# Idle TensorE matmuls regrouped and three small loads moved to another queue, in the head of an attention-and-MLP kernel

## The chip, the cores and the metric

One core of a Trainium2 chip runs the whole program. The metric is the device time of one execution in microseconds (us); unless it says otherwise, a number is the median of several executions. The profile's span is about 2 us shorter than the device time (297.5 against 299.37 for the profiled execution of the kernel before). In the clock records of these traces TensorE's granted clock is either 1.00 or 0.50; "the clock gate is open" means 1.00, "closed" 0.50. In the views PE is TensorE, ACT is ScalarE, DVE is VectorE, POOL is GpSimd, and SP is SyncE, which only issues DMAs here.

## The reference

A linear attention with cosine position weights, whose output goes through a two-layer MLP:

```python
# q, k, v: (8, 8, 576, 64) fp32; w_in (512, 2048); w_out (2048, 512)
r = relu(x);  phi(x) = concat([r * cos_w, r * sin_w])        # 128 features per head
kv  = einsum('bhsf,bhsd->bhfd', phi(k), v)
num = einsum('bhsf,bhfd->bhsd', phi(q), kv)
den = einsum('bhsf,bhf->bhs', phi(q), sum_s phi(k)) + 1e-6
x   = (num / den).transpose(0, 2, 1, 3).reshape(4608, 512)
h   = x @ w_in
out = (h * sigmoid(1.702 * h)) @ w_out
```

## The kernel before

The tokens go through the MLP in nine blocks of 512. While the MLP of block i runs, the attention of batch i+1 is worked in between its matmuls. A batch has 576 tokens: four chunks of 128 and a tail of 64. Before block 0 stands a head in which only batch 0's attention can run. Nearly all loads are issued by GpSimd, which casts fp32 to bf16 on the way:

```python
for g in range(1, 4): load_w_in(g)
load_w_out(0)
for n in "qk":
    load_main(1, n)
    load_tail(1, n)          # 64 tokens of batch 1, cast to bf16 by GpSimd's queue
load_w_out(1)
load_main(1, "v")
load_tail(1, "v")
load_w_out(2); load_w_out(3)
load_all(2)                  # q, k, v of batch 2, the last of the first stream of loads
```

Idle matmuls on a zero tile keep TensorE (PE) busy while it waits:

```python
warmup(14)                   # 14 idle matmuls of 512 columns
...                          # k prepared; two chunks of q prepared and transposed on PE
kv_lo = mm_tile()
for _ in range(6):
    nc.tensor.matmul(kv_lo, warm[:, 0:128], warm, start=True, stop=True)   # six more
kv_half(0, 0, kv_lo)         # k^T v of batch 0, heads 0 to 3
```

At the end of block 0 the attention result of batch 1 must be transposed (`x` to `xT`) before block 1 can start. Chunks 2 and 3 go through PE, the others through a DMA transpose on the SP queue:

```python
for c, k in enumerate(ks):
    at(k, unit_num, b, c)
    if i == 0 and c in (2, 3):
        at(min(k + 2, 31), turn_x_at, b, c)     # on PE, copied by ScalarE (ACT)
    else:
        at(k, turn_x, b, c)                     # nc.sync.dma_start_transpose(...)
```

## Time and profile before

| | before |
|---|---|
| device time | 300.03 us (299.83 to 300.39, 4 runs) |
| span | 297.5 us |
| first transposes of q on PE | 11.07 us |
| first numerator (needs k^T v) | 16.62 us |
| block 1 starts | 57.57 us |

One more place matters, and the prediction did not look at it: how block 1 starts. This is PE's timeline of the kernel before there (start, length, engine, line, operation, operands, count, and in brackets the idle time before it and what ended it):

```profile
56.51 0.39 PE L203 MATMUL at<-ident,xb 128*128 128x128 bf16 x4
57.57 0.81 PE L251 MATMUL mm<-xT,w_in_sb 128*128 128x512 bf16 x3 [0.67 <-ACT xT L205]
```

These are the two DMA transposes of x, chunks 0 and 1 of batch 1, in the view of one source line (count, duration on the issuing queue in ns, first and last start in us, and the time from issue to landing):

```profile
L208 SPq DMA_TRANSPOSE xT<-xb x1: 1192/1192/1192, 52.0 to 52.0; - x1
DMA to landing us min/median/max: 3.4/3.4/3.4
...
L208 SPq DMA_TRANSPOSE xT<-xb x1: 1702/1702/1702, 53.2 to 53.2; - x1
DMA to landing us min/median/max: 4.1/4.1/4.1
```

The second one lands at 57.4 (53.23 + 4.15, unrounded). The profile names ACT's copy as what released block 1 at 57.57, but this transfer landed only 0.2 us earlier.

### The profile page before, as it was taken

The page shows a single profiled execution, that of the slowest core. Times are in us where ns is not written, and L with a number is a line of the kernel's source. Part 1 is how long each engine was busy: PE and PEld are TensorE (multiplying, and loading weights), DVE is VectorE, ACT ScalarE, POOL GpSimd, SP SyncE. Part 2 cuts the span into 40 slices and gives each one's busy share as a digit, 9 for nine tenths or more (in the row PEclk, how much of TensorE's full clock was granted, in tenths as well). Part 3 has the DMA queues.
Part 4 walks back from the last instruction along what each step waited for, and adds up shares of the span by engine and source line. Part 5 has one row for each costly group of instructions (what it writes and reads, how often), then busy time and mean ns, then how long its engine had stood idle before and what let it go on. Part 6 is the DMA issues. An engine that isn't in the chain of part 4 may idle for free.

```text
span 297.5 us, 4997 instructions
## 1 busy us (share of the span) xinstructions
PE 284.1 (96%) x1930; PEld 143.7 (48%) x1930; DVE 105.0 (35%) x349; ACT 119.6 (40%) x203; POOL 101.1 (34%) x116
## 2 busy tenths in 40 slices
PE   6588999899999999999999999999999999999994
PEld 2364455445544554455445544554455444444443
DVE  3850547851581158114821482148214200000000
ACT  5546610464126511751165116511651167127411
POOL 8541520492269015800590159004501200120021
PEclk9599999999999999999999999999999999999999
DMA  8999999889969965897799889994902710111033
GB/s 193 196 204 194 196 201 192 175 198 161 164 137 189 186 106 138 180 187 104 147 183 168 123 101 181 177 164 119 192 0 54 126 42 0 39 71 35 2 68 73
DMA packets 90935, 39.91 MB, mean 134 GB/s; under 512 B 59744, under 2 KB 88672, under 8 KB 90912
## 3 DMA queue, kind: packets, MB, share of 16 engines
q0 software_dynamic: 42896, 26.88, 60.2%
q1 hardware_dynamic: 47856, 12.59, 21.5%
q8 instruction: 15, 0.25, 0.3%
q10 hardware_dynamic: 160, 0.13, 0.2%
q14 instruction: 8, 0.07, 0.1%
HBM read 36.70 MB, written 9.44 MB: 155 GB/s over the span
## 4 chain that ended last, share of the span: by engine, by line
PE 92%; DMA 3%; DVE 2%; ACT 1%; SPq 0%; issue 0%; DVEq 0%
PE mm L251 41%; PE mm L286 40%; PE at L235 3%; PE at L215 3%; DMA vt<-in_v_dram 3%; PE mm L310 1%; PE mm L358 1%; PE mm L328 1%; DVE xb L243 1%; PE mm L375 1%; ACT xT L354 1%; PE at L197 1%; PE mm L352 0%; DVE inv L242 0%; SPq L86 0%
## 5 line engine op out<-in xcount | busy, mean ns | idle before, releaser
L286 PE MATMUL mm<-w_out_sb,g 128*128 128x512 bf16 x560 | 129.0, 379 | 0.0
L251 PE MATMUL mm<-xT,w_in_sb 128*128 128x512 bf16 x564 | 124.3, 379 | 0.7 <-ACT xT L205 0.7
L298 POOL DMA_DIRECT2D out_dram<-ysb x54 | 56.0, 1042 | 170.9 <-ACT ysb L296 169.5
L256 ACT ACTIVATE g<-mm 128x512 bf16<-128x512 f32 x144 | 85.6, 597 | 46.2 <-PE mm L251 45.7
L251 PEld LDWEIGHTS <-w_in_sb 128*128 128x128 bf16 x564 | 54.7, 98 | 65.2 <-issue 0.8
L286 PEld LDWEIGHTS <-g 128*128 128x128 bf16 x560 | 52.0, 98 | 56.6
L296 ACT COPY ysb<-mm 128x512 f32<-128x512 f32 x34 | 19.9, 586 | 111.9 <-PE mm L286 111.9
L219 DVE CAST kvs<-at 128x260 bf16<-128x260 f32 x14 | 5.4, 426 | 59.2 <-PE at L215 59.2
L243 DVE TENSOR_TENSOR xb<-at,inv 128x512 bf16<-128x512 f32 (+1 forms) x36 | 24.8, 689 | 1.2
L241 DVE TENSOR_SCALAR den<-at 128x8 f32<-128x8 f32 (+1 forms) x36 | 5.9, 165 | 52.0 <-PE at L235 52.0
L315 DVE COPY ysb<-mm 128x256 f32<-128x256 f32 x1 | 0.4, 424 | 59.4 <-PE mm L310 59.4
L235 PEld LDWEIGHTS <-qT 128*128 128x128 bf16 x280 | 13.5, 98 | 8.3 <-DVE xb L243 0.3
L235 PE MATMUL at<-kvs,qT 128*128 128x65 bf16 x280 | 14.6, 193 | 0.1
L181 DVE TENSOR_SCALAR kp<-k,cosw 128x512 bf16<-128x512 bf16 (+1 forms) x32 | 11.6, 370 | 3.7 <-DMA k<-in_k_dram 3.7
L215 PEld LDWEIGHTS <-kp 128*128 128x128 bf16 x320 | 11.0, 98 | 2.2 <-issue 0.6
L181 DVE TENSOR_SCALAR qn<-q,cosw 128x512 bf16<-128x512 bf16 x32 | 11.3, 354 | 0.0
L181 DVE TENSOR_SCALAR qn<-q,sinw 128x512 bf16<-128x512 bf16 x32 | 10.8, 337 | 0.0
L215 PE MATMUL at<-vt,kp 128*128 128x65 bf16 x280 | 9.6, 193 | 0.0
L181 DVE TENSOR_SCALAR kp<-k,sinw 128x512 bf16<-128x512 bf16 x28 | 9.4, 337 | 0.0
L77 POOL DMA_DIRECT2D v<-in_v_dram x9 | 8.0, 887 | 4.1 <-DMA v<-in_v_dram 2.3
L77 POOL DMA_DIRECT2D q<-in_q_dram x8 | 7.9, 988 | 1.4 <-POOLq L470 0.8
L242 DVE RECIPROCAL inv<-den 128x8 f32<-128x8 f32 (+1 forms) x36 | 7.2, 201 | 1.2
(69 smaller groups left out, 119.4 us busy)
## 6 DMA issues: line engine op xcount, KB each, us to landing
out_dram<-ysb POOLq DMA_DIRECT2D x38, 128.0 KB, 2.8
q<-in_q_dram POOLq DMA_DIRECT2D x8, 512.0 KB, 9.1
out_dram<-ysb POOLq DMA_DIRECT2D x16, 256.0 KB, 3.1
k<-in_k_dram POOLq DMA_DIRECT2D x7, 512.0 KB, 11.0
v<-in_v_dram POOLq DMA_DIRECT2D x7, 512.0 KB, 12.5
w_out_sb<-in_moe_w_out_dram POOLq DMA_DIRECT2D x4, 512.0 KB, 15.2
w_in_sb<-in_moe_w_in_dram POOLq DMA_DIRECT2D x3, 512.0 KB, 13.8
k<-in_k_dram SPq DMA_DIRECT2D x1, 1024.0 KB, 6.0
```

The lines of the kernel that those rows point to most:

```text
L77: on.dma_start(out=state[b][n][:, 256 * h0:256 * h1].rearrange("p (h e) -> p h e", h=h1 - h0), in_=SRC[n][b, h0:h1, 0:512, :].rearrange("h ...
L181: nc.vector.tensor_scalar(oc, i, 0.0, wc, op0=MAX, op1=MUL)
L215: nc.tensor.matmul(kv[:, ds(h % 4 * (D + 1), D + 1)], kp[:, c, h, :], vt[:, c, h, 0:D + 1], start=(c == 0), stop=(c == NC - 1))
L235: nc.tensor.matmul(nm[:, h // 4, ds(h % 4 * (D + 1), D + 1)], q_slot(b, c)[:, h, :], state[b]["kvs"][:, h // 4, h % 4, 0:D + 1], start=Tru ...
L241: nc.vector.tensor_scalar(den[:r], nm4[:, :, :, D], 1e-6, None, op0=ADD)
L242: nc.vector.reciprocal(inv[:r], den[:r])
L243: nc.vector.tensor_tensor(state[b]["xb"][:r, c].rearrange("p (n h) d -> p n h d", n=2), nm4[:, :, :, 0:D], inv[:r].unsqueeze(3).to_broadca ...
L251: nc.tensor.matmul(hps[:, c0:c1], w_in_sb[:, kc, ds(fc * 128, 128)], xT[:, kc, ds(i * TB + c0, c1 - c0)], start=(kc == 0), stop=(kc == KC ...
L256: nc.scalar.activation(g, hps, AF.Gelu_apprx_sigmoid)
L286: nc.tensor.matmul(yps, gT[fc][:, ds(t * 128, 128)], w_out_sb[:, fc, :], start=(fc == 0), stop=(fc == FC - 1))
L296: nc.scalar.copy(ysb, cur[t])
L298: nc.gpsimd.dma_start(out=out[row:row + (n - 1) * step + 1:step, :], in_=ysb[p0:p0 + n, :])
```

## The change

Its intent: run idle matmuls right up to the first transposes of q, so that the clock gate stays open, take the six idle ones out of the way of k^T v, and take batch 1's tails off GpSimd's queue.

```diff
-            t = one.tile([64, 512], F32, name=n + "t0")
+            t = one.tile([64, 512], F32, name=f"{n}t{b}")
...
-    for n in "qk":
-        load_main(1, n)
-        load_tail(1, n)
+    load_main(1, "q")
+    load_main(1, "k")
     load_w_out(1)
     load_main(1, "v")
-    load_tail(1, "v")
...
-    warmup(14)
+    warmup(34)
...
     kv_lo = mm_tile()
-    for _ in range(6):
-        nc.tensor.matmul(kv_lo, warm[:, 0:128], warm, start=True, stop=True)
     kv_half(0, 0, kv_lo)
...
     turn_q(0, 4)
+    for n in "kvq":
+        load_tail(1, n, nc.sync)
```

## The prediction

> **What bounds the kernel now.** I read four views, in this order: the page's slices and chain, the timeline of the first 58 us, the windows of one microsecond through the head, and the landings of each load. The page first:
>
> ```profile
> span 297.5 us, 4997 instructions
> PE   6588999899999999999999999999999999999994
> PEclk9599999999999999999999999999999999999999
> DMA  8999999889969965897799889994902710111033
> PE 92%; DMA 3%; DVE 2%; ACT 1%; SPq 0%; issue 0%; DVEq 0%
> ```
>
> TensorE (PE) is full from the fifth slice (7.4 us each) to the last, and 92% of the chain that ended last is PE work. From 57.6 us on the chain is matmuls of blocks 1 to 8 with nothing between them. So only the head, 0 to 57.6 us, can move the end, and every microsecond won or lost there moves the end by one. The second digit of the granted clock, 5, says that something is wrong around 7 to 15 us. The timeline, PE alone, shows what:
>
> ```profile
> 1.19 5.17 PE L68 MATMUL mm<-warm 128*128 128x512 bf16 x14 [1.19 <-DVE warm L57]
> 11.07 1.89 PE L328 MATMUL mm<-ident,qn 128*128 128x128 bf16 x16 [4.71 <-DVE qn L181]
> 12.75 2.77 PE L375 MATMUL mm<-warm 128*128 128x512 bf16 x6
> 15.31 0.84 PE L215 MATMUL mm<-vt,kp 128*128 128x65 bf16 x20
> ```
>
> The columns are start, length, engine, line, operation, count, and the idle time before. The 14 idle matmuls (L68) end at 6.36; PE then sits idle for 4.71 us until q is prepared. The first transposes (L328) wait for VectorE (DVE), then six more idle matmuls (L375) stand in order ahead of k^T v (L215). The windows, granted clock in the third last column:
>
> ```profile
> 7.00:8.00 1.00, 0.00 (x0) 0.00 (x0) 1.00 (x2) 1.00 (x2) 0.92 (x2) 1.00 1.36 186
> 8.00:9.00 1.00, 0.00 (x0) 0.00 (x0) 1.00 (x4) 1.00 (x3) 0.00 (x0) 0.82 1.36 184
> 11.00:12.00 1.00, 0.93 (x9) 0.94 (x10) 0.92 (x6) 0.00 (x0) 0.97 (x2) 0.50 1.45 197
> 14.00:15.00 1.00, 1.00 (x4) 0.42 (x3) 0.03 (x1) 0.07 (x1) 1.00 (x2) 0.50 1.39 193
> 15.00:16.00 1.00, 1.00 (x23) 0.72 (x22) 0.00 (x0) 0.00 (x0) 0.40 (x2) 0.77 1.59 195
> 16.00:17.00 1.00, 0.98 (x25) 0.86 (x21) 0.00 (x0) 0.74 (x2) 1.00 (x2) 1.00 1.24 207
> ```
>
> The clock falls to half at 8.65 (finer windows) and comes back at 15.48. The transposes and all six idle matmuls run in that half-clock stretch; k^T v begins just as it ends.
>
> **What the Trainium skill says.** (1) "TensorE: Matmul & The Clock Gate", Part 1: activity over free-running windows of 3413 ns decides between half and full clock, and a 512-column matmul follows its predecessor by 426.7 ns cold and 215.7 ns warm. The trace agrees: half clock lasted 15.48 - 8.65 = 6.83 us, two such windows, after the release at 5.24 the gating came one window later (8.65), and the 24 matmuls of L286 from 82.65 took 5.18 us, 216 ns each, while the first idle ones repeat every 0.43. The window 5.24 to 8.65 was busy to (6.36 - 5.24)/3.41 = 33% and closed the gate; none at 70% or more did. (2) "DMA: Bandwidth & Descriptors", section "Issuing engines are not separate DMA queues": loads from any issuer share the same 16 engines and interleave. The trace agrees: 128 KB of v's tail from the SP queue took 7.98 us to land beside GpSimd's q. (3) "VectorE: DVE Perf Modes", "The perf-mode tier table": a one-input operation on SBUF is 4x in bf16, 2x in fp32. Here the k tail costs 0.47 us as fp32 (batch 0) and 0.34 us as bf16 (batch 1), so 0.13 us for 512 elements.
>
> **The change, part by part.**
>
> *Idle matmuls, 14 to 34.* In the traced phase the gate opens at 5.24, after (5.24 - 1.19)/0.427 = 9.5 of them; the other 24.5 take 24.5 x 0.216 = 5.3 us, so the run ends near 10.5, before q's first chunk is ready (11.02). The window 5.24 to 8.65 is now full, the next one is 0.5 us short of full, and the clock should stay at 1.00. The first transposes still start at 11.07 (DVE sets that), but the second group now takes warm time: an undisturbed group of 8 (L328, at 15.99) takes 0.46 from start to start, 0.65 to its copy's start. Second chunk ready at 11.54, so transposes issue until about 12.05 instead of 12.75.
>
> *Six idle matmuls removed.* That is 15.31 - 12.75 = 2.56 us of PE order. What binds next is v's first half: DVE copies it from 11.62 to 12.25. So k^T v starts near 12.3 instead of 15.31, and is done at 13.07. That 3.0 is not all kept, because ScalarE (ACT) has the two qT copies (L329, 0.96 each) first: 11.72 to 13.65 in the new order. Then kvs (0.38) at 13.65 instead of 16.19: 2.54 us earlier. From there I moved each piece of the before's chain with its own duration: third qT copy 14.03, first numerator 14.07, the fourth transposes 14.32, DVE's copy of them 14.97 instead of 17.52: 2.55. Its inputs are there: DVE is free at 14.03, v's second half landed at 12.9, the first w_in quarters at 14.2 and 15.5 against a first use at 21.23 - 2.5 = 18.7. So the head up to block 0's first matmuls gains **2.5 us**.
>
> *Tails of batch 1 on SP.* Three issues (0.7 us each) leave GpSimd, which wasn't the bound there; it waits for loads to finish. Three tails of 128 KB as fp32 go behind the transposing load of qT_tail on SP, at about 21.7 to 23.8. In the packet records each tail has 512 packets of about 31 ns as fp32 from SP and also as cast packets from GpSimd, so the DMA load is unchanged; it only comes earlier than q's main load, which I expect at about 31.6 instead of 30.4. DVE would start q of batch 1 up to 2 us later than it could, but PE asks for its first chunk only at 38.07 - 2.5 = 35.6, and that chunk is ready at about 32.3. On DVE, kt costs 2 x 0.13 more, vt 0.42 - 0.28 = 0.14, together 0.40. They stand ahead of k^T v of batch 1:
>
> ```profile
> 46.77 0.34 DVE L181 TENSOR_SCALAR kp<-kt,sinw 64x512 bf16<-64x512 bf16 x1
> 47.84 0.28 DVE L184 COPY vt<-vt 64x512 bf16<-64x512 bf16 x1
> 48.29 1.37 PE L215 MATMUL at<-vt,kp 128*128 128x65 bf16 x40
> ```
>
> DVE ends at 48.12 and PE begins at 48.29 without idling, so 0.15 is hidden and **0.25 us** comes back as a PE wait; after it the DVE-bound row of denominators and products (50.84 to 55.3) moves along. qt's 0.26 falls where DVE has room.
>
> *The transpose of qT_tail.* Issued at 22.92, landed 6.9 us later at 29.8, used at 30.26: 0.44 us of slack. Now all shifts by 2.5, but the transposing packets meet w_out (1024-byte packets, 98 ns) rather than q (512 bytes, 59 ns). With packets of both queues taking turns, 512 of them take about (98 + 31)/(59 + 31) of their 2.3 us, 3.2: 0.9 later against 0.44 of slack less scatter. I book **0.2 us** as a PE wait, between 0 and 0.5.
>
> *Sum, traced phase:* 2.5 - 0.25 - 0.2 = 2.05. The phase of the windows against the start varies from run to run. If the first gate opens later than 6.3, the 34 matmuls end after 11.07 (at an opening of 7.5: 14.8 cold, 19.2 warm, end at 11.65) and hold up the transposes by up to 0.8; half of the phases do, so about 0.2 on average. 2.05 - 0.2 = 1.85; 300.08 - 1.85 = **298.2 us**.
>
> **Rivals.**
>
> *The gate closes again later.* Without the six idle matmuls, and if transposes count for little (the skill's Part 4 of the same page says transposing matmuls do not count as busy the same way), a window after 12.04 could fall under the threshold; the next 3.4 us would run cold, at a cost of 1 to 2 us: time 299.5 to 300.3. For it: real matmuls cover some 50% of the windows 12.04 to 15.45 and 15.45 to 18.87 in my shifted order. Against it: the before's window 22.3 to 25.7 has much the same mix (0.8 us transposes, 1.6 us others) and stays at 1.00. I give it 1 in 10.
>
> *A landing takes the place of the wait.* The SP tails delay qT_tail, or q's main load, past their use. For it: DMA is saturated from 3 to 53 us (share 1.2 to 1.5) and qT_tail has the smallest slack of all. Against: tails stand behind it on the same ring, and other loads have 4 us or more. It would make 299 to 300. 2 in 10.
>
> *Idle matmuls overshoot.* 34 is more than fits if the clock opens late; 0.8 us at worst: 298.9.
>
> *More is gained.* No DMA trouble and an unfavourable phase in the before: 3 us, 297.
>
> **Range and chances.** The gain lies between 0.8 and 3.0 us in most of these; none comes near 6 us either way, which is what 2% would need. So 297.2 to 299.4, and within 2% is as good as certain.
>
> **What would show each step.** Right: granted clock 1.00 in every window from 5.3 (or the first opening) to the end; L328 from about 11.07; L215 at 12.3 with its releaser DVE's vt; kvs at 13.7, held by ACT's two copies; the first L358 at about 18.7; L235 of qT_tail with a small idle of PE; L215 of batch 1 about 2.3 us earlier with a 0.2 us wait for DVE; block 1's first L251 near 55.5 instead of 57.57. Wrong: a clock of 0.50 after 12 us, idle matmuls that still run at 11.1, a PE wait over 0.5 us for qT_tail, or for q of batch 1.

## The result, and the profile after

| | before | after |
|---|---|---|
| device time | 300.03 us (299.83 to 300.39, 4 runs) | 302.84 us (302.68 to 303.71, 4 runs) |
| ratio of the fast runs | | 1.0098 (95% interval 1.0076 to 1.012) |

A ratio is the mean time of one kernel's fast runs over that of the other's of the same rounds, so it is not quite the ratio of the medians. Executions over 1.5% slower than the fastest of the same kernel are left out of the means. The change made the kernel slower by 2.8 us, within 2%, and above the predicted range. The page after:

```profile
span 300.7 us, 4993 instructions
PE   8779999499999999999999999999999999999994
PEclk9999999989999999999999999999999999999999
DMA  8999999999589985999599968964902610011032
PE 87%; DMA 5%; ACT 3%; issue 1%; DVE 1%; SPq 0%; ACTq 0%; DVEq 0%
```

The 5 in the second slice of the clock is gone. In its place PE has a hole (4) in the eighth slice, 52.6 to 60.1 us, and the clock an 8 in the ninth. DMA has grown from 3% to 5% of the chain. PE's timeline in the head:

```profile
1.19 8.91 PE L68 MATMUL mm<-warm 128*128 128x512 bf16 x34 [1.19 <-DVE warm L57]
11.78 1.15 PE L326 MATMUL mm<-ident,qn 128*128 128x128 bf16 x16 [1.68 <-DVE qn L179]
12.76 0.87 PE L213 MATMUL mm<-vt,kp 128*128 128x65 bf16 x20
14.70 0.41 PE L333 MATMUL at<-kvs,qT 128*128 128x65 bf16 x8 [0.35 <-ACT kvs L217]
```

The head did what it was meant to: the first numerator (L333) starts at 14.70 instead of 16.62, although q landed 0.7 us later in this execution (transposes at 11.78, not 11.07). Then block 1 (L249 is L251 of before):

```profile
54.84 0.39 PE L201 MATMUL at<-ident,xb 128*128 128x128 bf16 x4
58.83 0.58 PE L249 MATMUL mm<-xT,w_in_sb 128*128 128x512 bf16 x1 [3.60 <-issue]
```

PE finished block 0 at 55.2, 1.7 us ahead of the before, and then stood for 3.6 us. The profile names no releaser ("issue"), but the view of the transposes' line names the waiter:

```profile
L206 SPq DMA_TRANSPOSE xT<-xb x1: 2017/2017/2017, 50.3 to 50.3; - x1
...
  PE mm L249: 3.6, 1
...
DMA to landing us min/median/max: 6.8/6.8/6.8
...
L206 SPq DMA_TRANSPOSE xT<-xb x1: 1237/1237/1237, 52.4 to 52.4; - x1
...
DMA to landing us min/median/max: 6.3/6.3/6.3
```

They were issued 1.7 and 0.8 us earlier than in the before and landed 1.7 and 1.4 later, at 57.1 and 58.7. Block 1 starts as the second lands. And the windows around it (granted clock in the third last column):

```profile
56.00:58.00 2.00, 0.00 (x0) 0.00 (x0) 2.00 (x9) 0.00 (x0) 1.82 (x1) 1.00 1.12 270
58.00:60.00 2.00, 1.17 (x3) 0.43 (x4) 2.00 (x8) 0.00 (x0) 2.00 (x1) 0.67 1.20 234
60.00:62.00 2.00, 2.00 (x6) 0.73 (x5) 2.00 (x10) 0.60 (x1) 2.00 (x1) 0.50 1.26 283
```

While PE stood, the clock gate closed: half clock from 58.7 to 62.1. So block 1 started 1.26 us later than before (58.83 against 57.57) and its first 3.3 us ran at half clock, which costs up to 3.3 x 0.5 = 1.6 us more. Together that is 2.9, against 2.8 between the medians (the two traced executions differ by 3.2). The questions for the chip: is the slow clock worth that much, which part of the change delays the transposes, and is it the stream of loads that they wait for?

### The profile page after: what moved, and what is told of

Same layout as the page of the kernel before. It is cut to its first block, busy times and chain, and to the rows that moved or that the text cites. A ratio compares the mean times of both kernels' runs of the same rounds, so it can differ in the third digit from the quotient of the medians.

```text
span 300.7 us, 4993 instructions
## 1 busy us (share of the span) xinstructions
PE 284.8 (95%) x1909; PEld 144.2 (48%) x1944; DVE 106.1 (35%) x349; ACT 119.4 (40%) x203; POOL 98.4 (33%) x113
## 4 chain that ended last, share of the span: by engine, by line
PE 87%; DMA 5%; ACT 3%; issue 1%; DVE 1%; SPq 0%; ACTq 0%; DVEq 0%
PE mm L249 40%; PE mm L284 38%; PE at L233 3%; DMA vt<-in_v_dram 3%; PE at L213 3%; DMA xT<-xb 2%; ACT g L254 1%; PE mm L308 1%; PE mm L356 1%; ACT xT L352 1%; PE at L195 1%; ACT qT L327 1%; PE mm L350 0%; PE mm L326 0%; SPq L86 0%
## 5 line engine op out<-in xcount | busy, mean ns | idle before, releaser
L249 PE MATMUL mm<-xT,w_in_sb 128*128 128x512 bf16 x548 | 125.1, 382 | 4.4 <-issue 3.6
L284 PE MATMUL mm<-w_out_sb,g 128*128 128x512 bf16 x542 | 126.7, 379 | 0.6
L254 ACT ACTIVATE g<-mm 128x512 bf16<-128x512 f32 x144 | 85.6, 597 | 50.8 <-PE mm L249 50.3
L249 PEld LDWEIGHTS <-w_in_sb 128*128 128x128 bf16 x564 | 55.0, 99 | 69.4 <-issue 5.9
L213 PEld LDWEIGHTS <-kp 128*128 128x128 bf16 x320 | 10.9, 97 | 1.8
L68 PE MATMUL mm<-warm 128*128 128x512 bf16 x34 | 8.9, 428 | 1.2 <-DVE warm L57 1.2
```

The source lines that it names most:

```text
L68: nc.tensor.matmul(wps, warm[:, 0:128], warm, start=True, stop=True)
L213: nc.tensor.matmul(kv[:, ds(h % 4 * (D + 1), D + 1)], kp[:, c, h, :], vt[:, c, h, 0:D + 1], start=(c == 0), stop=(c == NC - 1))
L249: nc.tensor.matmul(hps[:, c0:c1], w_in_sb[:, kc, ds(fc * 128, 128)], xT[:, kc, ds(i * TB + c0, c1 - c0)], start=(kc == 0), stop=(kc == KC ...
L254: nc.scalar.activation(g, hps, AF.Gelu_apprx_sigmoid)
L284: nc.tensor.matmul(yps, gT[fc][:, ds(t * 128, 128)], w_out_sb[:, fc, :], start=(fc == 0), stop=(fc == FC - 1))
```

## The experiments

Theory A: the DMA transposes of x are slow while the stream of loads runs, the stream's end sets block 1's start, and the fp32 tails on SP make the stream end later. Theory B: the idle-matmul part itself does harm. Other rivals (C: the transposes are slow for a reason of their own; D: the tails' place and not their cost; E: the tails cost only VectorE time) come with the runs that tell them apart. The runs of e1 to e4 were made together, so were e5 to e8, e9 and e10, and e11 and e12, each group on another chip; in these four groups the before's median was 300.24, 300.07, 300.27 and 300.06.

### e1: the idle-matmul part alone

```diff
 # kernel before
-    warmup(14)
+    warmup(34)
...
-    for _ in range(6):
-        nc.tensor.matmul(kv_lo, warm[:, 0:128], warm, start=True, stop=True)
```

> Only the idle-matmul part of the change (34 up to the first transposes, none ahead of k^T v); the tails of batch 1 stay with GpSimd. Theory A (block 1 waits for the DMA transposes of x, and these wait for the end of the load stream, which the fp32 tails made later): the last load of batch 2 lands near 55 as in the before, PE reaches the end of block 0 some 2.3 us sooner but block 1 still starts near 57.3 because of the transposes; time 299.5 to 300, at most 0.5 below the before. Theory B (the idle-matmul part itself hurts, by the clock or by the earlier order): time near 302.8 as in the full change.

Measured: 300.95 us (299.22 to 301.55), ratio 1.0008 (0.9982 to 1.0035). PE's timeline at block 1:

```profile
57.49 1.82 PE L251 MATMUL mm<-xT,w_in_sb 128*128 128x512 bf16 x4 [2.55 <-DMA xT<-xb]
```

PE was 2 us early, waited 2.55 us for the DMA transposes, and block 1 started where it starts in the before (57.57). The last load of batch 2 landed at 54.7 (before: 54.8), the second transpose at 57.4. That is theory A's picture. Its time came out above the 299.5 to 300 that I expected because I had left out the gate: in the traced execution it closed from 57.6 to 61.0, and from its start to block 2's, block 1 took 31.79 us (30.10 in the before). The one run whose mean clock was 1.00 took 299.22; the other five, at 0.992 to 0.994, took 300.66 to 301.55. So this half of the change gains nothing on its own: the wait is only moved, and the standing PE can lose its clock.

### e2: the tails alone

```diff
 # kernel before, with the tile names, load order and SP loads of the change
-        load_tail(1, n)          # for q, k; and for v
+    for n in "kvq":
+        load_tail(1, n, nc.sync)
```

> Only the other part: the before with the tails of batch 1 as fp32 on SP's queue. Theory A: the load stream ends some 2 us later, near 57; PE is at the end of block 0 as in the before (55.9 plus some 0.3), block 1 starts near 58.8 to 59.3; time 301.3 to 302.5, with the clock gate closing or not depending on the phase. Theory B: time within 0.4 of the before's 300.0.

Measured: 301.51 us (300.83 to 303.63), ratio 1.0045 (1.0009 to 1.0081). Block 1 started at 59.58, in the forecast's range for the time and nearly for the start; the stream ended at 55.9, where I had expected about 57, and the second transpose landed at 59.5. In the traced execution the gate also closed later in the head than in the before (10.9 to 17.8 against 8.6 to 15.5), so PE's own path was late too and ended at the same moment; this run speaks for A but does not prove it alone.

### e3: the change, with all four chunks of x transposed on PE

```diff
-                if i == 0 and c in (2, 3):
+                if i == 0 and c < 4:
```

> The full change, with x of chunks 0 and 1 of batch 1 also transposed on TensorE, as chunks 2 and 3 are, so that no DMA transpose stands between block 0 and block 1 but the tail's, which landed 20 us before. Theory A: block 1 starts 56.0 to 56.6, the clock stays at 1.00, time 298.0 to 299.2. Theory B (something else in the late head, such as the output stores, or the clock, holds PE): still over 301.5.

Measured: 298.92 us (298.80 to 299.63), ratio 0.9951 (0.993 to 0.9972). Block 1 started at 56.73 behind ACT's last copy, with no wait for DMA, and the clock was full:

```profile
56.73 1.46 PE L249 MATMUL mm<-xT,w_in_sb 128*128 128x512 bf16 x6 [0.67 <-ACT xT L203]
```

The one edit takes back 3.9 us of the changed kernel's 302.84 (2.8 of the 301.75 that it took when run again, e12): the waits for the transposes, and what followed from them, are the whole loss. Theory B is out.

### e4: the change, with 16 idle matmuls ahead of block 1

```diff
+        if i == 1:
+            warmup(16)
         for n in range(32):
```

> The full change with 16 idle matmuls ahead of block 1, where PE waited 3.6 us: they hold up nothing unless they outlast the wait, and they keep the activity up. If the closed gate (half clock from 58.7 to 62.1 in the trace) costs what half clock for one window costs, 3.4 x 0.5 = 1.7 us come back: 301.0 to 301.4. If the gate is harmless: 302.8.

Measured: 301.03 us (300.63 to 301.50). The idle matmuls ran 54.85 to 58.47 and the second transpose landed at 58.5:

```profile
54.85 3.62 PE L68 MATMUL mm<-warm 128*128 128x512 bf16 x16
58.54 1.67 PE L249 MATMUL mm<-xT,w_in_sb 128*128 128x512 bf16 x7
```

Block 1 begins at nearly the same moment as in the changed kernel, but at full clock. The difference, 302.84 - 301.03 = 1.8 us (2.4 by the two ratios, as the runs are of different rounds), is the price of the closed gate. The traces show it alone: from block 1's start to block 2's they have 58.83 to 90.52, or 31.69 us, in the changed kernel and 58.54 to 88.64, or 30.10, in e4 (30.10 in the before, too). That is 1.6 us.

### e5 and e6: k and v of batch 2 loaded later

```diff
-    load_all(2)
+    load_main(2, "q")
+    load_tail(2, "q")
...
         if i == 0:
+            for n in "kv":
+                load_main(2, n)
+                load_tail(2, n)
             evac(i, 3, nc.vector)
```

e5 is the full change with this edit, e6 the idle-matmul part with it.

> The full change, with k and v of batch 2 issued after the stores of block 0 (some 55 us) instead of at 32 to 41 us. Theory A (the DMA transposes of x wait for the end of the load stream): the stream now ends with q's tail of batch 2 near 49.5, both transposes land within 3.5 us of their issue (before 55), block 1 starts where PE and ACT bring it, 55.9 to 56.2, the gate stays open, time 297.9 to 298.7. Rival C (the transposes are slow for a reason of their own, such as the two in a row or the stores): they still land near 57 and 58.7, time over 301.

> Only the idle-matmul part, with k and v of batch 2 late as in the run before: a candidate to beat both kernels. Theory A: block 1 starts 55.6 to 56.0, time 297.7 to 298.4, 0.2 to 0.4 under the same with the tails on SP (what fp32 costs DVE). Rival C: 300.5 to 301, as the idle-matmul part alone.

Measured: e5 300.51 us (299.91 to 303.68, five fast runs; a sixth, 305.37, was slow), ratio 1.0038 (1.0 to 1.0076), e6 300.01 us (299.18 to 300.96). On the transposes theory A was right: in e5 the first landed 2.3 us after its issue (6.8 in the changed kernel) and the second, issued some 1.3 later, 3.6 after its own; block 1 started at 56.60 and 56.24, released by ACT. Rival C is out. On the time I was wrong, because the loads were now too late for block 1:

```profile
68.42 0.59 PE L214 MATMUL at<-vt,kp 128*128 128x65 bf16 x3 [0.44 <-DVE vt L183]
```

In e5, PE waits for VectorE's (DVE's) vt in k^T v of batch 2 (two more waits follow, 0.8 us in all), and DVE in turn waited for v's load. From its start to block 2's, block 1 took 31.72 us in e5 and 31.58 in e6 instead of 30.10, at full clock; so the late loads cost 1.5 to 1.6 us there. Why one fast execution of e5 took 303.68 stays open. e5's trace also holds the prediction's first rival: the gate closed in the head, from 19.2 to 22.6, after a window of 3.4 us in which PE was busy 58% of the time.

### e7: the idle-matmul part, with all four chunks transposed on PE

The edits of e1 and of e3, on the kernel before.

> Only the idle-matmul part, with x of chunks 0 and 1 of batch 1 transposed on TensorE: the other candidate. Theory A: as e3 (298.9), less what the fp32 tails cost DVE (0.25): 298.4 to 299.0. If the tails on SP had another cost in the head, more.

Measured: 298.92 us (298.51 to 299.81), ratio 0.9966 (0.9949 to 0.9983), block 1 at 56.67. It equals e3, which has the tails on SP besides. With no DMA transpose between the blocks the tails cost nothing that these runs can show; but the intervals of the two ratios are 0.5 to 0.6 us wide to each side, so the 0.25 us I had given them is not excluded.

### e8: the change, with each fp32 tail loaded twice

```diff
     for n in "kvq":
         load_tail(1, n, nc.sync)
+        twice = one.tile([64, 512], F32, name=n + "again")
+        nc.sync.dma_start(out=twice..., in_=<the same tail>)
```

> The full change with each fp32 tail of batch 1 loaded a second time into an unused tile from SP. My estimate from the packet records is 0.8 to 0.9 us of the whole stream for each fp32 tail: the last load of batch 2 lands near 59.3 instead of 56.8, block 1 starts some 2.5 us later, time 305 to 305.5. Rival D (not the bytes but the place of the tails and the order of the issues made the stream late): the end of the stream moves by less than 0.8, time under 303.8.

Measured: 303.45 us (302.42 to 304.40), not the 305 expected. The stream's end moved to 58.6, against 56.4 on average with single tails: 2.2 us later, so the cost of the loads themselves is real and rival D fell on that point. The time lies under D's 303.8, but it does not test D cleanly. q's tail came fifth of six and landed at 40.9, so DVE was late and PE stood much earlier than planned:

```profile
42.50 1.01 PE L195 MATMUL at<-ident,qn 128*128 128x128 bf16 x8 [3.02 <-DVE qT L196]
```

With that wait the gate closed, from 41.6 to 48.5, so PE's own path was late and met the transposes: they landed by 61.5, and block 1 started at 62.0, released by ACT.

### e9: the kernel before, with all four chunks transposed on PE

> The before with x of chunks 0 and 1 of batch 1 transposed on TensorE and nothing else, to be set against e7 (the same with the idle-matmul part). In e3 and e7 the two transposes on PE and their copies on ACT put the start of block 1 some 0.7 later than PE's own path. If the before was held only by that path: block 1 near 58.2, time 300.4 to 301, and e7's 298.9 is then 1.5 to 2.1 of gain from the idle-matmul part, its size where nothing hides it. If the before was held by the DMA transposes as well, by more than a few tenths: 299.5 or less.

Measured: 300.82 us (300.57 to 301.25), ratio 1.0017. Block 1 started at 58.60, released by ACT. The transposes on PE cost the before half a microsecond: it was held by PE's path, as the profile said, with the DMA only just hidden. Against e7 the idle-matmul part is now worth 300.82 - 298.92 = 1.9 us (1.5 by the two ratios), and block 1 starts 58.60 - 56.67 = 1.93 earlier. The gain that was predicted for the head is there as soon as nothing hides it.

### e10: the idle-matmul part, with v alone of batch 2 late

```diff
-    load_all(2)
+    for n in "qk":
+        load_main(2, n)
+        load_tail(2, n)
...
         if i == 0:
+            load_main(2, "v")
+            load_tail(2, "v")
             evac(i, 3, nc.vector)
```

> Only the idle-matmul part, with v alone of batch 2 issued after block 0's stores (e6 moved k too, and then PE waited for v at 67.8). Theory A: the load stream ends with k's tail of batch 2 near 51.5, the first DMA transpose lands near 53.5 and the second near 55.6, block 1 starts 55.6 to 56.3, v's tail of batch 2 lands before 65 and nothing waits for it in block 1: 297.8 to 298.7, below both kernels. If v is still too late: 299.5 to 300, as e6.

Measured: 297.38 us (297.35 to 297.40, 4 runs), ratio 0.99 (0.9886 to 0.9913). This beats both kernels: 2.9 us below the before of its rounds. The transposes and block 1:

```profile
L210 SPq DMA_TRANSPOSE xT<-xb x1: 1191/1191/1191, 50.1 to 50.1; - x1
DMA to landing us min/median/max: 2.3/2.3/2.3
...
L210 SPq DMA_TRANSPOSE xT<-xb x1: 1265/1265/1265, 51.3 to 51.3; - x1
DMA to landing us min/median/max: 3.7/3.7/3.7
```

```profile
55.66 1.67 PE L253 MATMUL mm<-xT,w_in_sb 128*128 128x512 bf16 x7 [0.67 <-ACT xT L207]
```

Both land by 55.0, block 1 starts at 55.66, and v's tail lands at 63.8, early enough. The gate stayed open from 4.9 us to 295.0 of the 295.5, and the four runs lie within 0.05 us.

### e11: e10 and the tails on SP; e12: the changed kernel once more

> The full change with v of batch 2 late: e10 plus the tails of batch 1 as fp32 on SP, so that the two differ by the tails alone. Theory A (fp32 tails on SP lengthen the load stream, and the DMA transposes wait for its end): the stream now ends with k's tail of batch 2 near 53.0 instead of 51.4, the transposes land near 54.5 and 56.5 instead of 52.4 and 55.1, block 1 starts 56.4 to 57.1 instead of 55.7, time 298.0 to 298.9. Rival E (the tails cost only their 0.25 to 0.4 on DVE): 297.6 to 297.8, with the transposes as in e10.

> The changed kernel unaltered, on the same chip and in the same rounds as e11. 302.5 to 303.2 if the gate closes before block 1 in all runs, as it did in the four runs so far; with a phase that keeps it open, a run near 301.

Measured: e11 297.91 us (297.66 to 299.04), ratio 0.9939; e12 301.75 us (300.40 to 303.06), ratio 1.007. In e11 the stream (now up to k's tail) ended at 52.7 (53.0 expected), 1.4 us later than in e10, but the transposes landed at 53.2 and 55.2, before PE's path needed them at 55.6. So the time missed A's forecast and lies just above rival E's: where the stream ends early enough, a longer stream is hidden, and the tails cost 0.5 us by the medians, or 0.7 with each median set against the before of its own rounds.

e12 shows two kinds of executions of the changed kernel: three from 300.40 to 300.98 and three from 302.52 to 303.06. The traced one is of the first kind, its clock was full throughout, and here the profile names the releaser:

```profile
58.07 1.24 PE L249 MATMUL mm<-xT,w_in_sb 128*128 128x512 bf16 x5 [3.15 <-DMA xT<-xb]
```

Without the closed gate, with a wait of 3.15 us, this kind takes some 2 us less. The gate's windows stand at another place against the program in each execution (it first opened between 4.06 and 6.57 us), so a wait of about 3 us closes it in some and not in others. Steps of 3.41 us, the distance of the clock's changes, show how: in the first trace of the changed kernel the step 55.26 to 58.67 lay wholly inside the wait, with PE busy 0%, and the gate closed; in e12's the wait fell into two steps with PE busy 43% and 63%, and it stayed open.

### What set the start of block 1

Times in us of the traced executions. "Stream" is the landing of the last load before block 1.

| kernel | stream ends | first transpose, issue to landing | second lands | block 1 starts | gate at block 1 |
|---|---|---|---|---|---|
| before | 54.8 | 52.0 to 55.4 | 57.4 | 57.57 | open |
| e1 | 54.7 | 50.0 to 55.2 | 57.4 | 57.49 | closed |
| after | 56.9 | 50.3 to 57.1 | 58.7 | 58.83 | closed |
| e12 (after) | 56.9 | 50.0 to 57.3 | 58.0 | 58.07 | open |
| e4 | 56.7 | 50.1 to 56.8 | 58.5 | 58.54 | open |
| e11 | 52.7 | 50.0 to 53.2 | 55.2 | 55.59 | open |
| e10 | 51.3 | 50.1 to 52.4 | 55.0 | 55.66 | open |

Issued at nearly the same time (50.0 to 50.3), the first transpose lands near the end of the stream, wherever that is. Issuing earlier didn't help. The packet records show where most of the delay is: the first packet of the transposes starts 1.2 us after the issue in the before, e10 and e11, but 2.6 us after it in e1 and 3.5 to 3.8 in after, e4 and e12.

Why do the tails lengthen the stream? Counts of DMA packets in half a microsecond, over all 16 engines, from the packet records of the traces (by the packets' starts, on the clock of the views):

```
after,  46.5: GpSimd's queue 192 x 512 bytes                    | SP's queue none
after,  28.0: GpSimd's queue 121 x 512 bytes                    | SP's queue 119 x 256 bytes (fp32 tail)
before, 49.5: GpSimd's queue 112 x 512, 243 x 128 bytes (a cast tail) | SP's queue none
```

Sixteen engines have 8 us in each half microsecond. My estimate from these counts: a 512-byte packet takes 8000/192 = 42 ns; with equal numbers of each kind a pair takes 8000/120 = 67, so the fp32 tail's packet takes 25 ns; the cast tail's takes (8000 - 112 x 42)/243 = 14. Three tails of 512 packets come to 1536 x 11 / 16 = 1.1 us more. The stream's end came 1.9 us later (56.42, the mean of after, e2, e3, e4 and e12, against 54.56 for before, e1, e7 and e9). I did not find the other 0.8. It is not the same in all pairs: without the two DMA transposes the end comes 1.3 to 1.4 later (e3's 55.7 against 54.3 and 54.4 in e7 and e9), with both issued at 50.0 to 50.3 2.1 later (56.8 in after, e4 and e12 against 54.7 in e1). So the transposes may slow the end of a longer stream in their turn; no run tests that.

## Why the prediction was wrong, point by point

- **The head's gain of 2.5 us**: right. The gate stayed open in the head (e5's trace is the exception), the first transposes ran at full clock, k^T v waited for v and kvs for ACT's two copies. The first numerator started at 14.01 in e12 against 16.62 in the before, with the tail of v landing at the same 10.0: 2.6 us. Between e9 and e7 1.5 to 1.9 us of it reached the time.
- **DVE's 0.40, of which 0.25 shows**: right in place. In the changed kernel DVE ended vt at 46.69 and PE had started at 46.47, with its group stretched from 1.37 to 1.53 us (1.67 in e12, after a wait of 0.14). As a loss of time it can't be seen between e3 and e7, while e11 and e10 differ by 0.5 to 0.7.
- **qT_tail, 0 to 0.5 us**: right, though (98 + 31)/(59 + 31) of 2.3 us is 3.3 and not 3.2. PE idled 0.10 to 0.55 us for it in five of the traces, and less than that or not at all in the others, the changed kernel's first trace among them.
- **"so the DMA load is unchanged; it only comes earlier"**: wrong. I equated packets by their duration of 31 ns each and did not ask what each takes from the 16 engines. The stream ended 1.9 us later.
- **"after it the DVE-bound row of denominators and products (50.84 to 55.3) moves along", and block 1 "near 55.5"**: this is the step that failed. I moved the instructions of block 0's end by 2 us and let block 1 follow, and dismissed all landings but qT_tail and q with "other loads have 4 us or more". I had listed the loads but not the two DMA transposes of x. Their second landing, at 57.4, left 0.2 us of slack in the before, and in these runs it moved with the end of the stream and not with the moment of issue. So block 1 could start no more than about 0.2 us earlier (57.49 in e1 against 57.57), and the later stream turned the win into a loss of 1.26 at block 1's start in the traced executions.
- **Rival 1, the gate closes again**: right in kind, and given 1 in 10 for another place. It closed in the new wait at block 1, at a price of 1.6 to 1.8 us (e4), in the traced one of the first four runs, and by their times in three of e12's six. The other three of the first four have a mean clock of 0.986, which is about 8 us at half clock each; where these lay is not recorded. Whether transposes count for less in it, no run shows: e5's window that ended with a closed gate and e3's that did not were both busy 58% of the time, 23% with transposes.
- **Rival 2, a landing takes the place of the wait**: the right mechanism with the wrong transfer. I bounded it at 300; with the gate on top it is 302.84.
- **Rival 3, idle matmuls overshoot**: in e1 and e4, where the gate first opened at 6.38 and 6.57, they ran right up to the transposes, which began at 11.40 and 11.44; in the changed kernel's two traces they ended 1.68 and 0.23 us before them. So it played no part in the loss.

## What to carry to other kernels

When a change shifts a stretch of work, list everything that the next stretch waits for, DMA transposes included, with its slack in the old trace; what the profile names as the releaser is only the last to come, and another may have come a fifth of a microsecond before it. A small transfer issued during a saturated stream may land when the stream ends, so shorten what stands before it rather than issue it sooner (e10 is e1 with v of batch 2 moved behind the transposes: 300.95 became 297.38). A wait of 3 us on TensorE can cost 1.6 to 1.8 us more in closed clock than it shows as idle time.

## What the Trainium skill lacked or had wrong

- "DMA: Bandwidth & Descriptors", section "DMA Transpose (X-bar)": it gives no latency for a small transpose beside a running stream. Here a transpose of one 128 x 512 chunk took 2.3 us from issue to landing in e10 and 6.8 us while the stream of loads ran.
- The same page, section "Queues, rings and completion order", has an engine take a whole packet of some 9 to 17 descriptors from one queue before it turns to the next, but does not say what share each of two busy queues gets. In these traces' records they moved equal numbers of entries, 121 of 512 bytes and 119 of 256 in the same half microsecond; so, by the estimate above, 256-byte entries took 25 ns each from a stream of 512-byte ones that take 42. How many entries an engine takes in a row the counts do not show.
- "TensorE: Matmul & The Clock Gate", Part 1, gives the window but not how much activity keeps the gate open. Here it closed after windows with PE busy 0% (after, e2), 25% (e1), 33% (before), 36% (e8) and 41% (e9) of the time, and once at 58% (e5), and stayed open at 43% (e12), 50% (e2) and 58% (e3, e11, e12); so no single share of busy time from the profile decides it.
